# RWKV linear attention and a two-layer MLP on one core: the first ten units in another order on all engines

## The chip, the core and the metric

The kernel runs on one core of a Trainium2 chip. The core has five engines that run their own instruction queues and wait for each other by semaphores: TensorE (PE in the profile, with its weight loads as PEld), VectorE (DVE), ScalarE (ACT), GpSimd (POOL) and SyncE (SP), which here only starts transfers. ACT and POOL start transfers too. SBUF is the working memory, PSUM the memory that TensorE writes.

The metric is the device time of one execution, in microseconds (us). Three runs of the kernel before took 186.01, 186.36 and 188.03 us, median 186.36.

## What is computed

The reference is a linear attention with a decaying state, followed by two matrix products with a SiLU between them:

```python
# r, k, v: (4, 8, 768, 48) f32; w, u: (8, 48)
for t in range(768):
    cur = einsum('bhd,bhe->bhde', u[None] * kt, vt)
    y[:, :, t] = einsum('bhd,bhde->bhe', rt, state + cur)
    state = w[None, :, :, None] * state + einsum('bhd,bhe->bhde', kt, vt)
x = y.transpose(0, 2, 1, 3).reshape(3072, 384)
h = x @ w_in              # w_in (384, 2048)
out = (h * sigmoid(h)) @ w_out   # w_out (2048, 384)
```

## The kernel before

**Units.** The 768 time steps are cut into six chunks of 128. A unit is one batch entry in one chunk, for all eight heads, so there are 24 units; unit i is batch i mod 4 of chunk i div 4. Units 0 to 3 (chunk 0) start from a zero state and are worked one by one. From unit 4 on two units are worked as a pair, and each chunk is taken as two halves of 64 steps (`in_halves`), with an inner state between the halves.

**One unit.** Three loads of 192 KB bring r, k and v (`ld`, L72; buffers `rin`, `kin`, `vin`, eight of each). TensorE turns r and k (`turn_one`, L255, to the PSUM tile `att`, of which there are two in turn); VectorE multiplies them with powers of the decay (`decay_one`, L270: `rT`, `kT`); TensorE multiplies them (`product`, L322, or `product_halves`, L395); VectorE masks the products (`am`, L328 or L402); TensorE makes the outputs from them and from v cast to 16 bits (`v16`, L246), plus the part from the carried state (L338, L484 to L501, PSUM tile `yp`). The term with u is added apart: `ku` = k * r (L223), `rku_f` = ku * u (L228), its sum over the head's columns `rku` (L236, VectorE), and `vu` = v * rku (L241). VectorE adds `vu` to `yp` and gives the 16-bit `y` (L343). The state: `kc` = k times a decay (L231), TensorE sums kc times v (`sp`; `first_sums`, L359, for units 0 to 3, `sums`, L418, later), and VectorE, ACT and POOL build the states and their layouts (`st`, `s1`, `sdec`, `s0p`, `s0h` and so on). Before, all of `ku`, `rku_f`, `kc` and `vu` run on POOL and all `v16` on ACT.

**The MLP.** y is turned to `xT`, by TensorE and a copy for units 0 to 5 (L531, L535) and by a DMA on SP's queue later (L524). The first layer (L546) goes by blocks of 128 of the 2048 columns, `ft` = 0 to 15, with three matmuls for each; SiLU is on ACT (L555, `gT`). A piece is one such block for the chunk's four units (three 512-column matmuls), or two blocks for two units (six 256-column ones). The second layer (L568) makes 128 x 384 outputs for a unit in four parts of four matmuls; ACT (for the last chunk VectorE) copies them out (L574, L576) and SP stores them. The weights come by eight casting transfers that POOL starts: `i_q0` to `i_q3` (L83) each bring a quarter of w_in, that is four blocks, and `i_o0` to `i_o3` (L88) a quarter of w_out.

**The order.** The schedule is manual: every engine runs its instructions in the order in which the program names them. For the first units that order is written out as a string of words (`order`), each a step with a unit or block number: `T2` turns unit 2, `kT2` decays its k, `ku2`, `ru2` and `vu2` are the products, `rd2` the sum, `n2` or `m4` a mask, `V2` and `e2` outputs and `y`, `S0` sums of units 0 and 1, `Q4` of 4 and 5, `D4` products of the pair 4 and 5, `Z4` its outputs, `L2.0` a first-layer piece with `G2.0` as its SiLU, `lk5` a load, `H` a half piece of chunk 1. `6*spin` issues six matmuls on zeros (L168, tile `zs`). Before, the string ends ahead of the sums of units 6 and 7. Then a loop takes the pairs, and `fill(n)` puts n pieces or parts of the MLP from the list `fillers` between the steps of the attention. All PSUM tiles but `att` share four buffers in turn (tag `moe`), so a tile waits until the one four before it is read.

Of the kernel before, what the change touches and what calls it, by code (L numbers as in the profile page):

```python
# [15 lines left out]
def kernel(  # L16
# [129 lines left out]

    lnwT = cst.tile([PR, NP], FP)
# [96 lines left out]
    def cast_v(i):  # L244
        L(i)["v16"] = wrk.tile([128, H, D], F16, name="v16", bufs=4)
        nc.scalar.copy(out=L(i)["v16"], in_=vin[i % NIN])  # L246
# [304 lines left out]
    def l1_silu(sc, b0, nb, ft):  # L551
        if sc not in gts:
            gts[sc] = wrk.tile([128, NFT, B * C], F16, name="gT", bufs=2)
        m = B // nb
        nc.scalar.activation(out=gts[sc][:, ft:ft + m, b0 * C:(b0 + nb) * C], in_=hpss[b0, ft],  # L555
                             func=AF.Silu)
# [7 lines left out]
    def l2_mm(sc, b, part):  # L564
        if part == 0:
            opss[b] = ps.tile([128, HD], FP, name="ops", tag="moe", bufs=4)
        for ft in range(4 * part, 4 * part + 4):
            nc.tensor.matmul(opss[b], gts[sc][:, ft, b * C:(b + 1) * C], wout[:, ft, :],  # L568
                             start=(ft == 0), stop=(ft == NFT - 1))

    def store(sc, b):
        osb = wrk.tile([128, HD], FP, name="osb", bufs=3)
        if sc < NCH - 1:
            nc.scalar.copy(out=osb, in_=opss[b])  # L574
        else:
            nc.vector.tensor_copy(out=osb, in_=opss[b])  # L576
# [39 lines left out]
    def rest_first(sc):  # L616
        return [lambda ft=ft: l1(sc, 2, 2, ft) for ft in range(0, NFT, 2)]

# [6 lines left out]
    begun = second(0)  # L625
    halved = [lambda ft=ft: l1(1, 0, 2, ft) for ft in range(0, NFT, 2)]

    def piece(word, f):
        b0, ft = word.split(".")
        f(0, *blocks[b0], int(ft))  # L630

# [8 lines left out]
        "tab": silu_table, "clear": clear, "spin": lambda: None, "H": lambda: halved.pop(0)(),  # L640
    }
    unit_steps = {
        "T": turn, "rT": lambda i: decay_one(i, 0), "kT": lambda i: decay_one(i, 1),
# [11 lines left out]
        "cg": lambda i: zero_state(i, nc.gpsimd),  # L655
    }
    order = """
        ur kz0 id itr lr0 wy pd0 ak0 cz2 kz3 itc wr mk wx cz1 mh lnw eK cg3 lamK kz4 kz1 lk1
        id16 lr1 pd3 lr3 lk3 clear 6*spin lv0 cg0 lv1 kz7 lr2 ak2 ku0 lv3 lr5 kz2 lv2 ub pd1 lv4
        lr4 lk4 lv5 pd2 lk5 lk7 lr6 lk6 uc T0 1*spin T1 lr7 lv7 kT0 pa4 rT0 ru0 ku1  # L660
        v160 pd5 lv6 rT1 kz6 rd0 kT1 wb ru1 P0 n0 2*spin rd1 P1 vu0 lnwb T2 n1 v161 2*spin
        pd7 lamC lamH pa6 i_q0 V0 v162 tab rT2 e0 kT2 ku2 T3 1*spin yT0 V1 kz5 vu1 i_q1 ru2
        xTD0 e1 P2 yT1 kT3 rd2 rT3 ku3 xTD1 P3 ru3 n2 rd3 v163 n3 L0.0 vu2 kc0 1*spin G0.0
        vu3 V2 L0.2 V3 G0.2 L0.4 e2 i_q2 e3 kc1 yT2 yT3 S0 G0.4 xT2 xTD3 kc2 L0.6 L2.4 G0.6
        st0 L2.0 scA0 v164 kc3 L2.6 ku4 i_q3 v165 L2.2 T4 rT4 kT4 G2.4 ru4 G2.2 T5 G2.0 G2.6
        L4.8 G4.8 L4.10 kT5 G4.10 L4.9 kc4 ku5 S2 L4.11 rd4 rT5 st2 sc2 kc5 sd4 ru5 G4.9
        G4.11 rA4 vu4 i_o0 Q4 D4 rA5 s1_4 ku7 L4.12 rd5 vu5 m4 s2_4 G4.12 L4.13 G4.13 T6 Z4
        L4.14 G4.14 L4.15 z4 yT4 2*spin yT5 i_o2 i_o1 ku6 xT4 xT5 rT6 T7 G4.15 rT7 v167 sd6
        kT6 v166 ru6 lr8 kc6 kc7 H H rd6 i_o3 H vu6 lr9 rP7 rA6 sn4 H H lk8 lk9 sx4 lv9 lv8
        ru7 kT7  # L670
    """
    for word in order.split():
# [5 lines left out]
        elif word[0] == "L":  # L678
            piece(word[1:], l1_mm)
        elif word[0] == "G":  # L680
            piece(word[1:], l1_silu)
        else:
            unit_steps[word[:-1]](int(word[-1]))
    fillers.extend(halved + begun)

    for i in range(B + 2, NU, 2):
# [7 lines left out]
        if i == B + 2:  # L694
            bonus_sum(i + 1)
            bonus_v(i + 1)
# [3 lines left out]
        if i > B + 2 or sc < NCH - 1:  # L700
# [55 lines left out]
```

## Time and profile before

| | |
|---|---|
| median of three runs | 186.36 us |
| the profiled execution's own time | 186.19 us |
| its span, first to last instruction | 184.5 us |
| mean granted clock of TensorE | 0.998 |
| TensorE, VectorE, ScalarE, GpSimd busy | 177.5, 115.9, 106.8, 112.1 us |
| read from and written to HBM | 20.45 and 4.72 MB |
| a load of r, k or v, issue to landing (median) | 3.9, 4.5, 4.3 us |
| a quarter of w_in, of w_out, issue to landing (median) | 6.0, 6.7 us |

A row of the profile's groups has line, engine, operation, what is written from what, count, then the busy time in us with the mean of one in ns, and then the engine's idle time just before and what ended it. The chain is the work that ended last, followed back from the end: start, length, what. In the timeline a row is start and length in us, engine, line, operation. A busy matmul can be one that only stands in the pipeline, so where TensorE's time is at stake the steps from start to start say more than the durations.

### The profile page before, as it was taken

The page shows a single profiled execution, that of the slowest core. Times are in us where ns is not written, and L with a number is a line of the kernel's source. Part 1 is how long each engine was busy: PE and PEld are TensorE (multiplying, and loading weights), DVE is VectorE, ACT ScalarE, POOL GpSimd, SP SyncE. Part 2 cuts the span into 40 slices and gives each one's busy share as a digit, 9 for nine tenths or more (in the row PEclk, how much of TensorE's full clock was granted, in tenths as well). Part 3 has the DMA queues.
Part 4 walks back from the last instruction along what each step waited for, and adds up shares of the span by engine and source line. Part 5 has one row for each costly group of instructions (what it writes and reads, how often), then busy time and mean ns, then how long its engine had stood idle before and what let it go on. Part 6 is the DMA issues. An engine that isn't in the chain of part 4 may idle for free.

```text
span 184.5 us, 6822 instructions
## 1 busy us (share of the span) xinstructions
PE 177.5 (96%) x2913; PEld 117.2 (64%) x2913; DVE 115.9 (63%) x226; ACT 106.8 (58%) x209; POOL 112.1 (61%) x148
## 2 busy tenths in 40 slices
PE   7987998999999999999999999999999999999993
PEld 2565785688666976756657656657656566555563
DVE  4799729786885855895845985946974954000120
ACT  3462788599124694268694268694377692299200
POOL 7999999997999439639558567579169030000000
PEclk9999999999999999999999999999999999999999
DMA  5999999899596386386295396293396201410022
GB/s 95 235 211 210 167 216 195 151 221 230 100 190 198 89 168 138 87 171 174 46 176 130 87 182 163 48 217 88 87 187 159 46 4 49 125 43 0 0 88 85
DMA packets 88594, 24.24 MB, mean 131 GB/s; under 512 B 83314, under 2 KB 88052, under 8 KB 88564
## 3 DMA queue, kind: packets, MB, share of 16 engines
q1 hardware_dynamic: 83952, 20.19, 50.3%
q0 software_dynamic: 2176, 3.15, 10.2%
q10 hardware_dynamic: 2436, 0.46, 1.3%
q8 instruction: 23, 0.38, 0.8%
q14 instruction: 7, 0.06, 0.1%
HBM read 20.45 MB, written 4.72 MB: 136 GB/s over the span
## 4 chain that ended last, share of the span: by engine, by line
PE 73%; POOL 17%; DMA 6%; issue 2%; ACT 0%; POOLq 0%
PE ops L568 33%; PE hps L546 26%; DMA kin<-in_k_dram 6%; PE att L395 4%; PE att L255 4%; POOL ku L223 4%; POOL kc L231 3%; POOL rku_f L228 3%; POOL vu L241 2%; PE yp L492 2%; PE sp L418 2%; PE ops L593 1%; POOL win L83 1%; PE yp L501 1%; POOL wout L88 1%
## 5 line engine op out<-in xcount | busy, mean ns | idle before, releaser
L546 PE MATMUL hps<-xT,win 128*128 128x512 f16 (+1 forms) x360 | 66.3, 337 | 0.3 <-DMA win<-in_moe_w_in_dram 0.3
L555 ACT ACTIVATE gT<-hps 128x512 f16<-128x512 f32 x96 | 56.0, 597 | 14.1 <-PE hps L546 10.6
L568 PE MATMUL ops<-wout,gT 128*128 128x384 f16 x368 | 62.5, 326 | 0.0
L546 PEld LDWEIGHTS <-win 128*128 128x128 f16 x360 | 38.9, 114 | 21.3 <-DMA win<-in_moe_w_in_dram 0.4
L568 PEld LDWEIGHTS <-gT 128*128 128x128 f16 x368 | 35.2, 98 | 23.3
L241 POOL TENSOR_TENSOR vu<-vin,rku 128x384 f32<-128x384 f32 x24 | 19.6, 831 | 22.7 <-DVE rku L236 22.6
L223 POOL TENSOR_TENSOR ku<-kin,rin 128x384 f32<-128x384 f32 x24 | 24.1, 1003 | 11.6 <-DMA kin<-in_k_dram 11.5
L270 DVE TENSOR_TENSOR rT<-att,lamR 112x512 f32<-112x512 f32 (+1 forms) x40 | 26.9, 682 | 4.2 <-PE att L255 3.8
L574 ACT COPY osb<-ops 128x384 f32<-128x384 f32 x20 | 9.6, 479 | 34.1 <-issue 18.1
L343 DVE TENSOR_TENSOR y<-yp,vu 64x384 f16<-64x384 f32 (+1 forms) x34 | 18.9, 555 | 16.1 <-PE yp L501 8.0
L228 POOL TENSOR_TENSOR rku_f<-ku,u_bc 128x384 f32<-128x384 f32 x24 | 24.1, 1003 | 1.5
L231 POOL TENSOR_TENSOR kc<-kin,lamH 128x384 f16<-128x384 f32 x20 | 20.1, 1007 | 0.0
L270 DVE TENSOR_TENSOR kT<-att,lamK 112x512 f32<-112x512 f32 x24 | 16.3, 681 | 0.1
L246 ACT CAST v<-vin 128x384 f16<-128x384 f32 x24 | 11.3, 510 | 7.8 <-DMA vin<-in_v_dram 7.5
L435 DVE TENSOR_TENSOR s<-sp,sdec 112x384 f32<-112x384 f32 x10 | 5.6, 558 | 16.1 <-PE sp L418 16.1
L576 DVE COPY osb<-ops 128x384 f32<-128x384 f32 x3 | 1.7, 558 | 21.3 <-PE ops L568 21.3
L402 DVE TENSOR_TENSOR am<-att,maskH 128x1024 f16<-128x1024 f32 x10 | 12.2, 1219 | 1.1 <-PE att L395 1.1
L236 DVE TENSOR_REDUCE rku<-rku_f 128x8 f32<-128x384 f32 x24 | 12.4, 543 | 0.0
L395 PE MATMUL att<-rT,kT 48*64 48x64 f32 x640 | 11.9, 220 | 0.5 <-issue 0.5
L374 ACT CAST s1h<-s 48x384 f16<-48x384 f32 x16 | 8.1, 509 | 5.4 <-DVE s L435 5.2
L395 PEld LDWEIGHTS att<-rT,kT 48*64 48x64 f32 x640 | 10.6, 135 | 0.7 <-issue 0.7
L255 PE MATMUL att<-ident,rin 64*112 64x64 f32 x192 | 10.0, 223 | 0.4 <-DVE rku L236 0.4
(92 smaller groups left out, 175.0 us busy)
## 6 DMA issues: line engine op xcount, KB each, us to landing
rin<-in_r_dram SPq DMA_DIRECT2D x24, 192.0 KB, 3.9
vin<-in_v_dram SPq DMA_DIRECT2D x24, 192.0 KB, 4.3
out_dram<-osb SPq DMA_DIRECT2D x23, 192.0 KB, 2.7
kin<-in_k_dram SPq DMA_DIRECT2D x22, 192.0 KB, 4.5
win<-in_moe_w_in_dram POOLq DMA_DIRECT2D x4, 384.0 KB, 6.0
wout<-in_moe_w_out_dram POOLq DMA_DIRECT2D x4, 384.0 KB, 6.7
kin<-in_k_dram ACTq DMA_DIRECT2D x2, 192.0 KB, 3.7
xT<-y SPq DMA_TRANSPOSE x18, 2.3
```

The source lines that it names most:

```text
L223: eng.tensor_tensor(out=L(i)["ku"], in0=kin[i % NIN][:, :, 0:D], in1=rin[i % NIN][:, :, 0:D], op=ALU.mult)
L228: eng.tensor_tensor(out=L(i)["rku_f"], in0=L(i)["ku"], in1=u_bc, op=ALU.mult)
L231: eng.tensor_tensor(out=kc[i % NIN][:, :, 0:D], in0=kin[i % NIN][:, :, 0:D], in1=lamH if in_halves(i) else lamC, op=ALU.mult)
L236: nc.vector.tensor_reduce(out=L(i)["rku"], in_=L(i)["rku_f"], axis=mybir.AxisListType.X, op=ALU.add)
L241: eng.tensor_tensor(out=L(i)["vu"], in0=vin[i % NIN], in1=L(i)["rku"].unsqueeze(2).broadcast_to([128, H, D]), op=ALU.mult)
L255: nc.tensor.transpose(L(i)["t"][0:PR, y, x, p, :], flat[rows, 128 * p:128 * p + PR], ident[rows, rows])
L270: nc.vector.tensor_tensor(out=L(i)[key].rearrange("p g (y t) -> p y g t", y=2), in0=L(i)["t"][0:PR, :, x], in1=lam, op=ALU.mult)
L343: nc.vector.tensor_tensor(out=y16[a], in0=y[b, 0:HD], in1=vu[a], op=ALU.add)
L395: nc.tensor.matmul(a[o0:o0 + HC, j, e, p, :], kT[r0:r0 + D, p, HC * x:HC * x + HC], rT[r0:r0 + D, p, HC * x:HC * x + HC], start=True, stop ...
L546: nc.tensor.matmul(hps[:, f, :], win[(ft + f) // 4].rearrange("p q (t c) -> p q t c", c=4) [:, q, :, (ft + f) % 4], xts[sc][:, q, b0:b0 + ...
L555: nc.scalar.activation(out=gts[sc][:, ft:ft + m, b0 * C:(b0 + nb) * C], in_=hpss[b0, ft], func=AF.Silu)
L568: nc.tensor.matmul(opss[b], gts[sc][:, ft, b * C:(b + 1) * C], wout[:, ft, :], start=(ft == 0), stop=(ft == NFT - 1))
```

## The change

The string of words is replaced by a longer one. It now goes to the hand-over ahead of the sums of units 10 and 11, and the loop starts at unit 10 instead of 6 (`2 * B + 2`). All that the loop did for units 6 to 9, and the filler pieces between, now stand in the string: `N` and `U` are half pieces of chunk 1 with their SiLU, `M` a part of the second layer, `O` a copy with its store, `yD` the turning by DMA, `rV` and `rW` the decayed r in 16 bits. When the loop starts, five of the 16 second-layer parts of chunk 1 are done (`second(1)[5:]`).

New words put operations on other engines: `kuD`, `ruD`, `kcD`, `vuD` run these products on VectorE (ku of units 3, 6, 8, 10; rku_f of 0, 4, 6, 8, 11; kc of 2, 7, 8; vu of 6, 10, 11), `v16D` casts v on VectorE (units 4, 5, 7, 8, 11), `rD` casts r there (5, 6; before on ACT), `ca` zeroes one state tile by copies on ACT. Two of the matmuls on zeros stay of 15. Unit 0 is loaded, turned and multiplied ahead of the rest, the sums of units 0 and 1 stand between the outputs of unit 0 and those of unit 1, and unit 3 comes ahead of 2. Quarters of w_in are asked for in the order 0, 3, 1, 2. The dictionaries of PSUM tiles get the chunk's number as a key.

```diff
+    def zero_state_copy(n):
+        t = (carry_pairs + inner_pairs)[n]
+        for e in range(2):
+            nc.scalar.copy(out=t[:, e].rearrange("p g n -> p (g n)"), in_=idle[0:PR, 0:NP * PW])
...
-    def cast_v(i):
+    def cast_v(i, copy=nc.scalar.copy):
...
-        hps = hpss[b0, ft] = ps.tile([128, m, nb * C], FP, name="hps", tag="moe", bufs=4)
+        hps = hpss[sc, b0, ft] = ps.tile([128, m, nb * C], FP, name="hps", tag="moe", bufs=4)
...
+        "kcD": lambda i: decayed_k(i, nc.vector), "vuD": lambda i: bonus_v(i, nc.vector),
+        "kuD": lambda i: bonus_ku(i, nc.vector), "ruD": lambda i: bonus_rku(i, nc.vector),
+        "v16D": lambda i: cast_v(i, nc.vector.tensor_copy), "rD": cast_r,
...
     order = """
-        ur kz0 id itr lr0 wy pd0 ak0 cz2 kz3 itc wr mk wx cz1 mh lnw eK cg3 lamK kz4 kz1 lk1
-        id16 lr1 pd3 lr3 lk3 clear 6*spin lv0 cg0 lv1 kz7 lr2 ak2 ku0 lv3 lr5 kz2 lv2 ub pd1 lv4
-        lr4 lk4 lv5 pd2 lk5 lk7 lr6 lk6 uc T0 1*spin T1 lr7 lv7 kT0 pa4 rT0 ru0 ku1
-        v160 pd5 lv6 rT1 kz6 rd0 kT1 wb ru1 P0 n0 2*spin rd1 P1 vu0 lnwb T2 n1 v161 2*spin
...
+        lr0 id pd5 clear wx cz0 pd7 cg3 kz7 ur mk pd2 lr1 ub lk1 wr wy pd6 lr3 itr kz0 lv0 ak0
+        itc pa1 lk3 kz4 kz1 pa0 lnw Ta0 Tb0 kz2 cz1 lv1 lk2 ku0 eK lamK wb lr2 uc mh ku1 rT0 Ta1
+        Tb1 lnwb ruD0 v160 kT0 lamC rd0 lv2 v161 P0 kT1 ru1 rT1 n0 pa3 vu0 P1 2*spin Ta3 id16
+        ca2 rd1 n1 Tb3 lk5 lamH i_q0 kT3 lr4 kc0 kuD3 kc1 tab rT3 ku2 V0 S0 Ta2 V1 pa4 e0 v162
+        Tb2 st0 vu1 e1 lv3 yT0 ru3 scA0 P3 xT0 lr5 yT1 kc3 kT2 ru2 rT2 xT1 i_q3 rd3 P2 v163 n3
+        L0.0 L0.2 kz3 vu3 Ta5 V3 rd2 lk4 G0.0 n2 V2 i_q1 vu2 Ta4 G0.2 kcD2 S2 e3 yT3 e2 yT2 Tb5
+        st2 lv5 xT3 scA2 i_q2 ku5 lv4 Tb4 xTD2 ru5 L2.0 L2.2 lk6 L4.12 lr6 kT5 L4.13 G2.0 G2.2
...
-    fillers.extend(halved + begun)
-
-    for i in range(B + 2, NU, 2):
+    fillers.extend(second(1)[5:])
+
+    for i in range(2 * B + 2, NU, 2):
```

More of the change, by code (lines that the diff above doesn't have):

```diff
@@ L663 @@
[L663 to L668, printed above, removed]
@@ L699 @@
             decayed_k(n)
-        if i > B + 2 or sc < NCH - 1:
-            next_state(i)
+        next_state(i)
         fill(4)
@@ L710 @@
         if b:
-            fillers.extend((first(sc) if sc > 1 else rest_first(sc)) + second(sc))
+            fillers.extend(first(sc) + second(sc))
         for n in nxt:
```

63 lines of the change are left out of this document (39 added, 24 removed).

## The prediction

> **What bounds the kernel now.** I read the page's busy times first, then the chain that ended last in order of time, then the stretches of 5 us, then each engine's timeline up to 72 us.
>
> ```profile
> PE 177.5 (96%) x2913; PEld 117.2 (64%) x2913; DVE 115.9 (63%) x226; ACT 106.8 (58%) x209; POOL 112.1 (61%) x148
> ```
>
> 96% for PE counts matmuls that are only pipelined or waiting, so it doesn't say where time is lost. The chain does:
>
> ```profile
> 47.59 0.44 PE att L255 x8
> 48.03 7.91 PE ops L568 x48
> ...
> 66.40 3.25 PE ops L568 x20
> 69.65 0.37 PE sp L418 x32
> ...
> 89.05 4.66 PE hps L546 x21
> 102.70 4.66 PE ops L568 x28
> ```
>
> From 47.59 us on every piece is PE and each starts where the last ends. Two prices come from here: 4.66/21 = 0.222 us for one 512-column matmul of the first layer (0.67 us for a piece, which is three of these or six of 256 columns), and 4.66/28 = 0.166 us for one of the second layer (0.66 us for a part of four). The first `sp` piece of units 10 and 11 is at 69.65 us. There the rewritten order hands over to the loop, which is the same in both kernels, except that the new order has done five of the 16 second-layer parts of chunk 1, the old one four. So the whole change is worth: 69.65 + 0.65 minus the time at which the new kernel reaches that `sp`.
>
> ```profile
> 5.00:10.00 5.00, 5.00 (x72) 3.04 (x71) 4.04 (x14) 1.56 (x5) 4.86 (x9) 1.00 1.18 238
> 10.00:15.00 5.00, 4.37 (x88) 2.95 (x88) 5.00 (x9) 2.92 (x8) 4.93 (x8) 1.00 1.16 198
> 15.00:20.00 5.00, 3.93 (x90) 3.18 (x86) 5.00 (x10) 2.62 (x4) 4.92 (x6) 1.00 1.24 218
> 20.00:25.00 5.00, 4.68 (x62) 4.16 (x61) 2.41 (x5) 3.16 (x7) 4.98 (x6) 1.00 1.04 158
> ```
>
> (PE, PEld, DVE, ACT, POOL busy in each stretch, then granted clock, DMA share, GB/s.) From 5 to 20 us DVE and POOL are both full, and PE waits for them. From 20 us on DVE has room, POOL has none until 40 us. DMA is full to about 45 us.
>
> ```profile
> 2.97 2.77 PE L168 MATMUL zs<-idle 128*128 128x512 f16 x6
> 9.93 0.60 PE L168 MATMUL zs<-idle 128*128 128x512 f16 x2
> 18.57 0.85 PE L546 MATMUL hps<-xT,win 128*128 128x256 f16 x6
> ```
>
> The first useful first-layer matmul (piece 0.0) is at 18.57 us. The dummies before it step at 0.43 us early on and at about 0.2 us later.
>
> **The prize.** From 18.57 to 69.65 us are 51.1 us. The work in it, at the chain's dense prices: 32 first-layer pieces 21.3; 20 second-layer parts 13.2; turns of eight units 8 x 0.52 = 4.2; five pairs of sums at 0.37 = 1.9; three product pairs at 0.98 = 2.9; outputs of units 4 to 9, 0.83 + 0.83 + 0.65 = 2.3; two outputs and four turned y of units 2 to 5, 1.3. That is 47.1 us: 4 us of it are dummies and waits. The new order has one pair of sums less in it and one part more, 47.4. If piece 0.0 stays where it is and PE never waits, the `sp` comes at 66.0 us, and the gain is 69.65 + 0.65 - 66.0 = 4.3 us. Only an earlier piece 0.0 could give more.
>
> **The moved operations.** Up to the hand-over 15 two-input products go from POOL to DVE (four `ku`, five `rku_f`, three `kc`, three `vu`), and seven casts from ACT to DVE.
>
> ```profile
> L223 POOL TENSOR_TENSOR ku<-kin,rin 128x384 f32<-128x384 f32 x24 | 24.1, 1003 | 11.6 <-DMA kin<-in_k_dram 11.5
> L343 DVE TENSOR_TENSOR y<-yp,vu 64x384 f16<-64x384 f32 (+1 forms) x34 | 18.9, 555 | 16.1 <-PE yp L501 8.0
> ```
>
> On POOL such a product takes 1.0 us. No row has it on DVE; nearest is `y`, as wide, 0.555 us, whose one input lies in PSUM. With both inputs in SBUF beside a POOL that reads SBUF all the time, nothing in this trace says whether the two run freely: `eK`, the only such DVE operation (0.69 us), ran beside memsets. So the bounds are 0.47 us (the step from one `y` to the next instruction) and 0.555 plus one whole POOL operation, 1.56 us. I take 0.555 plus half a POOL operation, 1.05 us, while POOL is full, as either engine comes at a random moment of the other's instruction and both ends of the range are equally far; free running is a rival. The casts: 0.35 us (`xT`) to 0.62 (ACT's `rT`), I take 0.4 to 0.6. By the Trainium skill (SBUF — State Buffer, Who interferes with whom) a DVE instruction with two SBUF inputs and a GpSimd instruction that reads SBUF block each other for a whole instruction; no run shown here has that pair. By that rule the held-up value stands, without it the rival's.
>
> **The walk** (steps between starts on DVE: decay 0.60, mask 1.15, reduce 0.46, `y` 0.5).
> *To piece 0.0.* Old: 18.57. In the new order `rku_f` of unit 0 stands on DVE ahead of `kT` of unit 0 and waits for POOL's `ku` (k0 is now the fourth DMA of ACT's queue, not the third, and lands at about 6.4 instead of 5.89, so `ku` ends at 7.45). Free: products of unit 0 at 8.65 (old 8.90), masks to 13.0, two decays, `ku` of unit 3, `y0`, state copy, `y1`, two decays to 17.5, products of unit 2, piece 0.0 at 18.6: no gain, since DVE is as full as before. Held up: 0.25 for `rku_f` behind the half mask, 0.5 for `ku`: 19.4, a loss of 0.8.
> *To piece 2.0.* DVE has both masks, `kc` of unit 2, `y3`, `y2`, state copy and `xT2`: free 23.25, held up 24.5 (0.5 more for `kc`). PE's work there (two pieces, two half turns, outputs, sums, turned y, two half turns) is 3.6 us, so 1.0 or 1.5 are lost.
> *To piece 8.* It needs w_in quarter 2, now asked for last: POOL's order puts quarters 3, 1, 2 at 19.6, 21.4 and 23.5 us (18.5, 20.2, 21.9 free; old: 25.1, 14.1, 20.5). One alone takes 5.4 us to land; when queued, they land 2.8 us apart (w_out: 38.56, 41.39, 44.23). Quarter 3 lands at 25.1, before its use at 25.9; quarter 2 at about 31.2 (free 30.0), while PE gets there at 30.2 (29.0): 1.0 lost. The other loads fill the DMA as before, about 0.9 us each; r6 and k6 are there by 31, needed at 34.7.
> *To the end of chunk 0's first layer.* After the turns of units 6 and 7 DVE has `ku6` and four decays ahead of the products, then three `y` ahead of the turned y: 0.5 lost free, 1.0 held up (40.6 us). All of w_out is asked for from 38.7 on; the first part needs it at 48.7.
> *Units 6 to 9.* `kc7`, two casts, mask and `rku_f` of unit 6 stand before the inner state of units 6 and 7: outputs wait 1.15 held up, about 0.1 free. Then `vu6`, three `y`, `kc8`, `ku8`, `rku_f` 8, seven decays end at 59.1 (55.3 free) against PE's 58.9 (55.9): 0.1.
> Everything else added sits under PE: POOL's `vu7` and `ku9` ahead of the third w_out quarter (asked for at 43.7, needed at 53.4), the DMA transposes behind loads on SP (needed one pair later). ACT loses seven casts, gains a zeroing, and was busy for 24.7 of the first 40 us. v3 stands behind k5 and r4 now and lands at about 18.4 (12.84 before; the fourteenth load of before landed at 18.46), in time for unit 3's outputs at 20 us.
>
> **Sum.** Held up: 0.8 + 1.5 + 1.0 + 1.0 + 1.15 + 0.1 = 5.6 lost of the prize of 4.3: 1.3 to 1.4 us slower, on the profiled execution's own 186.19 us: **187.6 us** (the median of the runs is 186.36). Free: 1.0 + 1.0 + 0.5 + 0.1 = 2.6 of 4.3, a gain of 1.7: 184.5. A chip can tell about 1% (1.9 us) of this kernel from no change.
>
> **Rivals.**
> *DVE and POOL run freely*: **184.5 us**, from 183.4 if quarter 2 also lands in time. For it: DVE has 19 us idle up to 70 us (50.9 busy), the added 10.5 fit, and POOL loses 14 us of work in its full stretch. Against: the first 20 us, where DVE has no room.
> *The clock of TensorE*: the first dummies step at 0.43 us, the pair at 9.93 at half that, although the granted clock reads 1.00 throughout; only work in between can have done that. The change takes away 13 of 15 dummies, the six at 2.97 us above all, and PE waits for r0, k0, r1. If PE is still slow up to 20 us, two pairs of products (1.03 each) double, one before the masks and one before piece 0.0 (1.0 + 1.1), and part of that hides behind quarter 2; two slow pieces add 1.3. That decides once PE's work between 3 and 9 us is too sparse: **189.7 us**. The Trainium skill (TensorE: Matmul & The Clock Gate, Part 1) puts the release after about 3.4 us of sustained activity and half the clock before it; the dummies agree (0.43, later 0.2).
> *What PE gains DVE loses*: half of the moved operations meet an idle POOL (it waits for `rku` of unit 7 and for k9 after 38 us), and the waits cancel the prize: 186.2, no change.
>
> **The numbers.** Held up 0.45, own range 186.0 to 189.5; free 0.27; slow clock 0.16; no change 0.12. Faster than 184.5 needs about half of the free case and a little from others' errors in the walk: 0.25. Slower than 188.2: most of the slow clock, a third of the held-up case, 0.34 with errors of the walk, which sees no small waits. In between 0.41. The range, 183.4 to 190.4, takes in the free case with its best end and the slow clock with 0.7 on top.
>
> **What would show it.** Right: piece 0.0 at 19 to 20.5 us; DVE's two-input products above 0.56 us or late beside a busy POOL; DVE full from 5 to 40 us; a wait for `win` of about 1 us near 30 us; `sp` of units 10 and 11 near 71.7 us, and the same length after it. Wrong: products at 0.55 us with nothing queued and `sp` by 68.5 us; transposes and products of units 0 to 3 twice as long as here; or a loop after the hand-over that no longer runs PE piece to piece.

## The result, and the profile after

| | before | after |
|---|---|---|
| median of the runs | 186.5 us (4 runs) | 193.19 us (4 runs, 192.7 to 194.41) |
| ratio after/before, 95% interval | | 1.0354 [1.0277, 1.0431] |
| the profiled execution's own time | 186.19 us | 193.1 us |
| its span | 184.5 us | 190.6 us |

The changed kernel is 3.5% slower. The sign is as forecast; the size is not: 193.2 lies beyond 183.4 to 190.4. The busy times of the page after (to set against those of before):

```profile
PE 178.9 (94%) x2900; PEld 118.8 (62%) x2900; DVE 133.0 (70%) x242; ACT 107.3 (56%) x210; POOL 101.0 (53%) x132
```

VectorE has 17.1 us more to do, GpSimd 11.1 less. Of VectorE's 17.1 only some 10.7 are the work of the 22 operations (15 times 0.55 and 7 times 0.35, the times with nothing beside them). The chain of after in order of time (start, length, what):

```profile
32.11 1.49 PE hps L551 x6
...
45.26 2.69 DVE rku_f L233
47.95 0.48 DVE s L440
...
62.08 1.16 PE att L400 x64
...
70.39 2.98 DVE rku_f L233
73.38 0.27 DVE v L251
...
75.95 1.16 PE att L400 x64
```

Before, this chain is TensorE from 47.59 us on. Now VectorE carries most of it from 34.75 to 76 us, with two products `rku_f` of 2.7 and 3.0 us that take 0.55 where nothing is beside them. That the chain runs through VectorE does not mean that TensorE stood still all that time. What TensorE waited for, its own timeline names:

```profile
48.47 0.20 PE L489 MATMUL yp<-s0p,rT 112*64 112x96 f16 x1 [1.41 <-DVE s L440]
49.53 0.26 PE L489 MATMUL yp<-s1p,rT 112*64 112x96 f16 x2 [0.86 <-ACT s1p L375]
62.08 1.16 PE L400 MATMUL att<-rT,kT 48*64 48x64 f32 x64 [0.45 <-DVE rT L275]
75.95 1.16 PE L400 MATMUL att<-rT,kT 48*64 48x64 f32 x64 [0.62 <-DVE rT L275]
```

With two waits for `y` (0.30 at 40.50 and 0.15 at 52.00) that is 3.8 us from 34.75 to 76 us, and none between 62.08 and the sums of units 10 and 11. From 75.95 us on TensorE runs from piece to piece as before. The same stretches as were shown of before (length of the stretch, then PE, PEld, DVE, ACT and POOL busy, granted clock, DMA share, GB/s):

```profile
5.00:10.00 5.00, 3.88 (x44) 2.50 (x46) 3.18 (x7) 2.50 (x6) 3.58 (x5) 1.00 1.15 229
10.00:15.00 5.00, 5.00 (x88) 3.73 (x84) 4.02 (x6) 4.49 (x11) 4.98 (x7) 1.00 1.05 194
15.00:20.00 5.00, 3.90 (x110) 3.12 (x108) 5.00 (x10) 2.27 (x6) 5.00 (x6) 1.00 1.03 189
20.00:25.00 5.00, 4.34 (x78) 3.31 (x76) 5.00 (x8) 1.77 (x4) 4.88 (x8) 1.00 1.13 194
```

From 20 to 25 us VectorE, 2.41 us busy before, is full; from 10 to 15, where it was full, it now has 1 us to spare, because TensorE is late. TensorE's timeline of after has the three marks:

```profile
9.40 3.67 PE L327 MATMUL att<-rT,kT 48*64 48x128 f32 x64
20.12 1.50 PE L551 MATMUL hps<-xT,win 128*128 128x256 f16 x12
74.90 0.44 PE L423 MATMUL sp<-v,kc 64*64 64x48 f16 x32
```

The products of units 0 and 1 take 1.84 us each (1.09 before): TensorE, with no dummies ahead of it, is slow until about 13.9 us. Piece 0.0 starts at 20.12 (18.57). The sums of units 10 and 11 come at 74.90 (69.58 in before's timeline). Of the 6.9 us between the two profiled executions 1.55 are there by piece 0.0, 3.77 more by these sums, 0.8 more up to the end of the span (products of units 10 and 11 wait 0.62 for `rT`), and 0.8 lie outside the span (2.5 us after, 1.7 before).

Two measures are used below: the time of piece 0.0, and the **stretch** from there to the sums of units 10 and 11, 51.01 us before and 54.78 after. Both are TensorE's starts in the timeline of the profiled execution.

### The profile page after: what moved, and what is told of

It reads as the page before. It is cut to its first block, busy times and chain, and to the rows that moved or that the text cites. A ratio compares the mean times of both kernels' runs of the same rounds, so it can differ in the third digit from the quotient of the medians.

```text
span 190.6 us, 6771 instructions
## 1 busy us (share of the span) xinstructions
PE 178.9 (94%) x2900; PEld 118.8 (62%) x2900; DVE 133.0 (70%) x242; ACT 107.3 (56%) x210; POOL 101.0 (53%) x132
## 4 chain that ended last, share of the span: by engine, by line
PE 62%; DVE 19%; POOL 7%; DMA 7%; issue 2%; ACT 0%; ACTq 0%; DVEq 0%; POOLq 0%
PE ops L573 25%; PE hps L551 24%; DMA win<-in_moe_w_in_dram 5%; PE att L400 4%; PE att L260 4%; DVE rku_f L233 3%; DVE rT L275 3%; DMA kin<-in_k_dram 2%; DVE y L348 2%; DVE kT L275 2%; POOL vu L246 2%; POOL ku L228 2%; DVE rku L241 2%; POOL kc L236 2%; PE ops L598 1%
## 5 line engine op out<-in xcount | busy, mean ns | idle before, releaser
L560 ACT ACTIVATE gT<-hps 128x512 f16<-128x512 f32 x96 | 56.7, 597 | 17.8 <-PE hps L551 14.0
L246 POOL TENSOR_TENSOR vu<-vin,rku 128x384 f32<-128x384 f32 x21 | 18.8, 910 | 31.0 <-DVE rku L241 31.0
L228 POOL TENSOR_TENSOR ku<-kin,rin 128x384 f32<-128x384 f32 x20 | 20.6, 1031 | 13.4 <-DMA kin<-in_k_dram 13.2
L233 POOL TENSOR_TENSOR rku_f<-ku,u_bc 128x384 f32<-128x384 f32 x19 | 19.0, 1002 | 7.3 <-DVE ku L228 6.1
L236 POOL TENSOR_TENSOR kc<-kin,lamH 128x384 f16<-128x384 f32 x18 | 18.5, 1029 | 0.0
L260 PE MATMUL att<-ident,kin 64*112 64x64 f32 x192 | 9.8, 225 | 1.1 <-ACT lamK L191 1.1
L260 PE MATMUL att<-ident,rin 64*112 64x64 f32 x192 | 10.6, 232 | 0.0
```

Of the source, the lines that this page charges most:

```text
L228: eng.tensor_tensor(out=L(i)["ku"], in0=kin[i % NIN][:, :, 0:D], in1=rin[i % NIN][:, :, 0:D], op=ALU.mult)
L233: eng.tensor_tensor(out=L(i)["rku_f"], in0=L(i)["ku"], in1=u_bc, op=ALU.mult)
L236: eng.tensor_tensor(out=kc[i % NIN][:, :, 0:D], in0=kin[i % NIN][:, :, 0:D], in1=lamH if in_halves(i) else lamC, op=ALU.mult)
L246: eng.tensor_tensor(out=L(i)["vu"], in0=vin[i % NIN], in1=L(i)["rku"].unsqueeze(2).broadcast_to([128, H, D]), op=ALU.mult)
L260: nc.tensor.transpose(L(i)["t"][0:PR, y, x, p, :], flat[rows, 128 * p:128 * p + PR], ident[rows, rows])
```

## The experiments

The theory: 22 operations on VectorE wait beside a full GpSimd. The rivals: the clock of TensorE without its dummies; the new order itself; VectorE's own added work.

### The disputed cost by itself

*e1.* VectorE's products, casts and products that read PSUM, alone and beside six GpSimd products in a row.

```diff
+    x = meet("two", x, [tt] * 4)       # both inputs in SBUF
+    x = meet("cast", x, [cast] * 4)
+    x = meet("psum", x, [from_psum] * 4)
```

> This kernel leaves the whole computation out. It times four VectorE operations of 128 x 384 f32 beside a run of six GpSimd products of the same size that follow each other without a wait: first alone, then (a) products with both inputs in SBUF, (b) casts from SBUF to SBUF, (c) products with one input in PSUM. The first VectorE operation of each set waits for the first GpSimd product. Shut out for the run: in (a) the first operation ends only when GpSimd's six are done, about 5 us after it could start, and the other three take 0.5 each after that; (b) likewise if the cast uses the shared port; (c) 0.55 each, beside the run. Half an operation, as the prediction priced it: in (a) each operation takes 0.6 to 1.6 us and the two engines take turns. Free: 0.55 us in (a), 0.35 in (b), with GpSimd at 1.0 throughout.

VectorE's timeline in e1, alone and then beside GpSimd:

```profile
2.45 0.55 DVE L46 TENSOR_TENSOR alonetwob<-b 128x384 f32<-128x384 f32 x1
9.30 1.34 DVE L46 TENSOR_TENSOR twob<-b 128x384 f32<-128x384 f32 x1
16.78 1.15 DVE L51 CAST castb<-b 128x384 f16<-128x384 f32 x1
23.54 0.55 DVE L56 TENSOR_TENSOR psumc<-acc,b 128x384 f32<-128x384 f32 x1
```

The two engines take strict turns: a VectorE product of 0.55 us takes 1.34, a cast of 0.35 takes 1.15, and GpSimd's products stretch from 0.99 to 1.31. With one input in PSUM nothing happens. This fits the Trainium skill (SBUF — State Buffer, Who interferes with whom), by which a VectorE instruction with two SBUF inputs and a GpSimd instruction that reads SBUF shut each other out for a whole instruction. It does not explain the changed kernel, where most of the 22 operations took little more than alone (0.55, casts 0.35) and three took 2.3 to 3.1 us.

*e5, e9, e13.* So GpSimd was given the kernel's own forms. e5:

```diff
+    x = meet("A", x, [decay] * 6, [two] * 4)
+    x = meet("G", x, [state, decay, decay, plain, decay, plain], [mid, two, mid, cast, mid, two])
```

> The whole computation is left out: VectorE and GpSimd run against each other in seven groups, and the output is no result of the reference. GpSimd's runs now have the kernel's own forms: A six products kc (float16 out, rows of 64), B six sdec, C six products with rku broadcast, D kc and the memsets of kc in turn and a sdec at the end, E six kc, F six plain float32 products, G sdec, kc, kc, plain, kc, plain as around the operation of 3.07 us. VectorE has four two-input products in A to C; in D to G its operations with two inputs or casts stand between operations that read PSUM, so that each arrives in the middle of a GpSimd operation. If the turn-taking of the run before (1.33 us each, one GpSimd operation waited for) holds for every form, all contending VectorE operations take 1.0 to 1.4 us, in E to G 0.6 to 1.5 by when they arrive, and none reaches 2 us. If a form of GpSimd's keeps VectorE out over its end (kc with float16 out, or the memsets between), A, D, E or G show operations of 2 to 3 us and B, C, F do not. If it is the arrival in the middle that loses a turn, F shows 2 us as well.

Groups A and C showed turns (1.34 and 1.18), E and F the rest of one GpSimd operation (0.86); in B one product of four missed a turn (1.96); the cast groups stayed under 1.15. In G, where a `sdec` leads, the first product took 6.39 us: it got in only when GpSimd's run was over. e9 varied the moment of arrival, with and without a `sdec` at the head of the run:

```diff
+    for state in (False, True):
+        for again in range(2):
+            for delays in ([], [64], [128], [192], [256], [320], [384], [448], [512], ...):
+                x = meet(x, state, delays)
```

> The whole computation is left out: 48 small groups in which GpSimd runs five two-input products in a row and VectorE brings one two-input product (0.55 us alone), after reads of PSUM whose width sets the moment: it arrives between 0.1 and 1.1 us after the start of GpSimd's run, in 12 steps, each step twice. In the first 24 groups the run consists of plain float32 products, in the last 24 it begins with a sdec. If the moment of arrival decides who waits how long, the wait follows the steps in the same way in both halves and in both repeats: one remainder of a GpSimd operation for most moments (0.6 to 1.3 us for the product), and 3 us or more for a narrow window of moments near the end of a GpSimd operation. If the sdec ahead of it is what shuts VectorE out, the first half shows nothing above 1.5 us and the last half does. If it is chance, the repeats differ.

VectorE's timeline in e9, the second arrival of twelve, in the first half and in the second:

```profile
11.00 1.13 DVE L68 TENSOR_TENSOR two<-a,b 128x384 f32<-128x384 f32 x1
...
195.11 5.71 DVE L68 TENSOR_TENSOR two<-a,b 128x384 f32<-128x384 f32 x1
```

In 24 of 24 runs of plain products it took 0.66 to 1.35, falling by 0.07 for each step of arrival and jumping back after an end: it waits for the end of one operation. In 24 of 24 runs that a `sdec` began it took 4.85 to 5.84: passed over at every end until GpSimd had nothing left, also when it arrived after the `sdec` was over. Neither the moment nor chance decides; GpSimd's run does. e13 asked what it is in the run:

```diff
+        for x_op in (plain, state, wide, short, spread, decay, clean, cast, ask):
+            x = meet(x, [x_op] + [plain] * 4, 1)
```

> The whole computation is left out: 16 groups, done twice over, of a GpSimd run with VectorE's two-input product arriving 0.35 us after the run's start. In the first nine the run is one operation X and then four plain products: X is a plain product, a sdec (112 partitions, second input broadcast), the same on 128 partitions, a plain product on 112 partitions, vu (128 partitions, second input broadcast), kc (float16 out), the memset of kc, a cast of 48 partitions, the request of a DMA. Then a sdec twice ahead of plain products, a sdec with one plain product between, a sdec ahead of kc; and four runs with a sdec, a vu or a DMA request in the middle against five VectorE products. The run before showed 0.66 to 1.35 us in runs of plain products and 4.85 to 5.84 us, to the end of the run, in all 24 runs that a sdec begins. If the number of partitions does it, the plain product on 112 shuts VectorE out and the sdec on 128 does not; if the broadcast input does it, the sdec on 128 and vu shut it out and the plain product on 112 does not; if it is any change of form between neighbours, vu, the memset, the cast and the DMA request ahead of plain products do so too, and kc perhaps. A VectorE product takes 0.6 to 1.4 us where it is let in at the next end of an operation and 4.5 us or more where it is not.

Both repeats agreed within 0.02 us except after a DMA request (1.73 and 1.60). The product took 0.99 behind a plain product, 0.82 behind the 128-partition `sdec` and behind `vu`, 1.03 behind the plain product of 112 partitions, 0.99 behind `kc`; but 1.77 behind the `sdec`, 1.44 behind a cast, 1.6 to 1.7 behind a DMA request: there it was passed over at one end. None of the three answers expected came out clean, and the wait to the end of the run did not come back, though the run of `sdec` and four plain products looks like that of e9. What decides how many ends are missed stays open.

### Moving the operations back

*e2* returned four of the operations that were held up longest, the casts of r of units 5 and 6 and `rku_f` of units 6 and 11:

```diff
-  rD5 ... rD6 ... ruD6 ... ruDB
+  rA5 ... rA6 ... ru6 ... ruB
```

> The new kernel with the four VectorE operations that took longest beside GpSimd put back: rku_f of units 6 and 11 on GpSimd, the casts of r of units 5 and 6 on ACT. If being shut out by GpSimd's run is what delays the chain: the outputs of units 6 and 7 start at about 47 us instead of 49.5, the products of units 10 and 11 don't wait, the sums of units 10 and 11 come at about 72.5 instead of 74.9 us, and the time is about 190.5 us, 2.5 less than the new kernel. If the order of the steps costs the time, whoever runs them: within 0.7 us of 193.

It took 191.83 us, ratio 1.0312 [1.025, 1.0374], 1.4 less than the changed kernel, where 2.5 were expected; its runs (190.88 to 193.66) overlap with those of the changed kernel. TensorE no longer waited for `s` near 47 us. VectorE's timeline shows why the rest did not come:

```profile
27.41 2.41 DVE L233 TENSOR_TENSOR rku_f<-ku,u_bc 128x384 f32<-128x384 f32 x1
...
45.97 3.09 DVE L246 TENSOR_TENSOR vu<-vin,rku 128x384 f32<-128x384 f32 x1
...
68.08 3.85 DVE L251 CAST v<-vin 128x384 f16<-128x384 f32 x1
```

These three took 0.55, 1.28 and 0.35 in the changed kernel. Other moved operations were shut out in place of those taken away.

*e4* returned all 22, in the new order. *e7* moved the same 22 in the old order.

```diff
 e4:  -ruD0 kuD3 kcD2 rD5 ruD4 v16D4 ...     e7:  -ru0 ku3 kc2 rA5 ru4 v164 ...
      +ru0 ku3 kc2 rA5 ru4 v164 ...               +ruD0 kuD3 kcD2 rD5 ruD4 v16D4 ...
```

> The new order, but all 15 products back on GpSimd and all seven casts back on ACT, so that VectorE has no operation that reads SBUF beside GpSimd except as before. If the moves to VectorE cost the time: 187 to 190 us, with sums of units 10 and 11 at 69 to 72 us, though GpSimd has 14 us more to do. If the order costs it: 193 or more, with GpSimd full to 55 us and w_out asked for late.

> The old order, with the same 15 products on VectorE instead of GpSimd and the same 7 casts on VectorE instead of ScalarE. If the moves cost by themselves (VectorE held up while GpSimd runs), the time is 188 to 190 us, with VectorE operations of 1.3 to 3 us and waits of TensorE for VectorE in the first 76 us. If they cost only in the new order, where VectorE has no room, it is 185 to 187, GpSimd being the engine that was full in the old order until 45 us.

| | operations as before | 22 moved |
|---|---|---|
| old order | 186.36 | 200.46, ratio 1.0751 [1.0702, 1.08] (e7) |
| new order | 189.85, ratio 1.0208 [1.0157, 1.026] (e4) | 193.19 |

Each part costs by itself: the order 3.5 us, the moves 3.3 us in the new order and 14 in the old one, where at most 4 were expected. Not all of the 14 is time held up: in e7 TensorE, kept waiting, also ran slow again (18 first-layer matmuls at 50.97 took 4.03 us, 2.15 at its usual step, and the granted clock was 0.50 from 50 to 55 us). In e7 the longest waits of the moved operations lie in two runs of GpSimd that begin with a DMA request (at 21.50 and at 25.20 us):

```profile
23.65 2.35 DVE L231 TENSOR_TENSOR kc<-kin,lamC 128x384 f16<-128x384 f32 x1
...
26.39 4.64 DVE L246 CAST v<-vin 128x384 f16<-128x384 f32 x2
```

So the new order leaves VectorE better places for the 22 operations than the old one does, but not good enough ones.

### The same work on VectorE, less beside it

To tell waiting from work, GpSimd's side was made lighter and VectorE's left alone. *e10* and *e11* made every GpSimd product a memset, in the changed kernel and in e4:

```diff
+        if eng is nc.gpsimd:
+            return eng.memset(L(i)["ku"], 1.0)
```

> The changed kernel with its 22 operations on VectorE as they are, and each product left on GpSimd, and each sdec, replaced by a GpSimd memset of the same tile (about 0.2 to 0.45 us instead of 0.8 to 1.0, and with no input to read); what these products compute is left out. VectorE's own work is the same as in the changed kernel. If the moves cost 3.3 us because VectorE is held up by GpSimd's products, its operations take 0.55 and 0.35 (up to 0.8 at most), and the kernel comes to within 1 us of the next one. If they cost because VectorE simply has 10 us more to do in a stretch in which it is full, it stays 2.5 to 3.3 us above the next one.

> The new order with the 15 products on GpSimd and the 7 casts on ScalarE (189.85 us in full), with the same replacement: every product and sdec on GpSimd is a memset, so what they compute is left out, those 15 included. It is the one to compare the run before with: the same order and dummies, no operation held up, and 10 us less work for VectorE. Both theories expect 187.5 to 189.5 here, by what GpSimd's lateness costs this order (1.5 us of waits for kc in the run without the replacement); slower than 190 would mean that the dummies and the order cost more than was taken.

Ratios 1.0345 [1.0266, 1.0425] and 1.0397 [1.0348, 1.0447]: no difference that the moves could have made, but this pair does not settle it, since both became slower than e4. GpSimd, with nothing to wait for, asked for the last three w_in quarters between 13.3 and 16.1 us (19.4 to 22.7 in the changed kernel), and TensorE then waited for r, 5.8 us in e11. What it did show: beside memsets all 15 moved products took 0.55 us.

*e14* and *e15* left out only five `kc`, the ones beside VectorE's three longest waits:

```diff
-  kc5 ... kc4 ... kc9 ... kcB kcA
```

> The changed kernel with five of GpSimd's products left out: kc of units 4, 5, 9, 10 and 11, which stand where VectorE's three longest waits were (2.27 us at 27.61, 2.77 at 45.19, 3.07 at 70.31). What they compute is left out: the sums of those units use an older kc or zeros, so the output is not the reference's. VectorE keeps all 22 moved operations. None of the five is waited for by the path of the changed kernel, so only what they did to VectorE is taken away. If those waits are what the moves cost, the three operations take about 0.6 to 1.3 us, the outputs of units 6 and 7 wait at least 1 us less, the sums of units 10 and 11 come 1.5 to 3 us before 74.90, and the time is 190.2 to 191.7. If VectorE's own added work is the cost, or the wait moves on to the next operation each time, it is 192.5 to 193.5.

> The same five kc left out of the kernel with the 15 products on GpSimd and the 7 casts on ScalarE (189.85 us with them), as the measure for the run before: what they compute is left out. No VectorE operation is held up here, so it should stay at 189.2 to 190.1; less would mean that GpSimd's work itself was late in this order, and only what the run before gains beyond that is the hold-up's.

e14 took 191.86 us, ratio 1.0285 [1.0232, 1.0338], e15 190.15, ratio 1.0212 [1.0177, 1.0248]: the gap of 3.3 us between changed and moved back shrinks to 1.7, and e15 stays where e4 was. VectorE's timeline of e14, the three operations of 2.27, 2.77 and 3.07 us:

```profile
28.10 0.45 DVE L311 CAST rT<-rT 112x512 f16<-112x512 f32 x1
...
44.85 1.81 DVE L233 TENSOR_TENSOR rku_f<-ku,u_bc 128x384 f32<-128x384 f32 x1
...
69.03 1.14 DVE L233 TENSOR_TENSOR rku_f<-ku,u_bc 128x384 f32<-128x384 f32 x1
```

*e17* and *e18* made all GpSimd products of units 4 to 11 memsets, and kept the w_in requests where they were:

```diff
+        return eng is nc.gpsimd and 4 <= i < 12
```

> The changed kernel with each product that GpSimd makes for units 4 to 11 replaced by a memset of the same tile (what they compute is left out); the products of units 0 to 3, each sdec, the DMA requests and all 22 moved operations stay, so that the w_in requests, which an earlier run moved with its memsets, keep their moments. In that earlier run no VectorE operation was held up beside memsets (0.55 and 0.42 us). If waiting beside GpSimd's products makes the whole 3.3 us between the changed kernel and the one with everything moved back, of which leaving out five products showed half, this run comes to within 0.8 us of the next one, whatever time that has. If the other half is VectorE's own 10 us of added work, it stays 1.3 to 2 us above it.

> The same replacement, units 4 to 11, in the new order with the 15 products on GpSimd and the 7 casts on ScalarE: the measure for the run before. What the replaced products compute is left out. VectorE is not held up here in full (189.85 us) either; 188.5 to 190.2 is expected, less only by what GpSimd's products are late for in this order.

Ratios 1.0226 [1.0165, 1.0286] and 1.038 [1.0291, 1.047]. The whole times do not compare: in e18's profiled execution TensorE was slow again from 18 to 25 us (units 2 and 3 multiplied in 1.97 us each), and piece 0.0 came at 22.60, its twelve matmuls in 2.62 us instead of 1.50. So a second, shorter stretch is set beside the first: from the start of piece 2.0, the next first-layer work, where TensorE is at full speed in all of these:

| to the sums of units 10 and 11, us | from piece 0.0 | from piece 2.0 |
|---|---|---|
| before | 51.01 | |
| all 22 moved back, with dummies (e8) | 51.92 | 46.13 |
| all 22 moved back, without five `kc` (e15) | 51.39 | 46.00 |
| all 22 moved back, units 4 to 11 memsets on GpSimd (e18) | 51.47 | 46.13 |
| changed | 54.78 | 49.57 |
| changed, five `kc` left out (e14) | 53.01 | 47.80 |
| changed, units 4 to 11 memsets on GpSimd (e17) | 52.42 | 47.49 |

(e4's own stretch, 53.16, is left aside: 21 first-layer matmuls at 25.90 took 4.95 us there, 3.44 in the others.) From piece 2.0 on the moves cost 3.4 us (49.57 less 46.13). TensorE's named waits account for 2.9 of them: it waits 0.82 for w_in, 0.30 and 0.15 for `y` and 1.41, 0.86 and 0.45 behind VectorE in the changed kernel, and 0.93 for w_in and 0.21 for `y` in e8. With five `kc` gone on both sides 1.8 of the 3.4 are left (e14 and e15), with memsets on both sides 1.4 (e17 and e18). What is left beside memsets is of another kind. TensorE's timeline of e17 names 0.28 us for w_in, 0.36 behind a cast of v that had itself waited 0.94 for its load, and this wait for a load of k:

```profile
47.54 0.44 PE L271 MATMUL att<-ident,kin 64*112 64x64 f32 x8 [0.76 <-DMA kin<-in_k_dram]
```

In e18, where TensorE gets there 3 us later, none of the three is there. VectorE's own work is the same in the changed kernel, e14 and e17. So waiting beside GpSimd's products is at least 2.0 of the 3.4 us, and no row names a wait that VectorE's own added work alone would explain.

### The dummies

*e3* put six dummies back in the changed kernel, *e6* took 13 of 15 from the old one, *e8* gave e4 sixteen, *e16* gave the changed kernel the same sixteen.

```diff
 e3:   id pd5 clear +6*spin wx cz0
 e6:   clear -6*spin lv0;  T0 -1*spin T1;  n0 -2*spin rd1;  T3 -1*spin yT0;  kc0 -1*spin G0.0;  yT4 -2*spin yT5
 e8 and e16:  clear +6*spin;  rT0 +1*spin;  P0 +4*spin;  ku2 +1*spin;  P3 +1*spin;  ahead of S2 +3*spin
```

> The new kernel with the six matmuls on zeros back behind the clearing of att, as the kernel before has them. If TensorE is slow because these are gone: the products of units 0 and 1 take about 2.1 us together instead of 3.67, the masks come 1 us earlier, piece 0.0 starts at about 19.1 instead of 20.1 us, and the time falls by 0.3 to 1.0 us (part of it is lost again in the wait for quarter 2 of w_in): 192.2 to 192.9. If the slow products have another cause: 3.67 us and 193.2 again.

> The old order and its old engines, with 13 of its 15 dummy multiplications taken away and nothing else. If the slow TensorE clock is what the order costs (the 3.6 us that are left when all products and casts are moved back), the products of units 0 and 1 take 1.5 to 2 us instead of 1.09, the transposes and first pieces are slow up to 20 us and more, piece 0.0 comes 1 to 1.5 us later than 18.57, and the time is 187.7 to 189.7 us. If the dummies do not matter (the clock comes up by itself before TensorE is the limit), it is 185.9 to 186.6.

> The new order with all 15 products on GpSimd and the 7 casts on ScalarE (189.85 us without more), and 16 dummy multiplications put back where TensorE is idle: 6 after the clearing of the banks, 1 before the transposes of unit 1, 4 after the product of unit 0, 1 before the outputs of unit 0, 1 after the product of unit 3, 3 before the sums of units 2 and 3. If the slow clock makes the order's 3.6 us, the products take 1.09 throughout, piece 0.0 comes at 18.6 to 19.3 and the time is 186.5 to 188. If the order costs by its late w_in quarters and its later first-layer pieces, it stays at 189 to 190.3.

> The changed kernel as it is, with 16 dummy multiplications at the places where they took 1.2 us off the kernel with everything moved back (6 after the clearing, 1 before the transposes of unit 1, 4 after the product of unit 0, 1 before the outputs of unit 0, 1 after the product of unit 3, 3 before the sums of units 2 and 3). If the six dummies of an earlier run failed (194.15 us) because the clock fell back in the sparse stretch behind them, the products take 1.09 us here up to piece 0.0 and the time is 191.6 to 192.6. If an earlier TensorE only brings the masks and casts of VectorE to worse moments beside GpSimd, it stays at 193 to 194.5, with the clock up.

| | time, us | ratio to before | piece 0.0 |
|---|---|---|---|
| e3, changed + 6 | 194.15 | 1.043 [1.0393, 1.0468] | 21.45 |
| e6, before - 13 | 186.94 | 1.0035 [1.0004, 1.0066] | 20.28 |
| e8, e4 + 16 | 188.62 | 1.0116 [1.0067, 1.0166] | 20.23 |
| e16, changed + 16 | 193.9 | 1.0419 [1.0371, 1.0466] | 20.12 |

In the old order the slow start brings piece 0.0 1.7 us later, as the rival said (e6: both products 1.84 us), but only 0.7 us of it is left at the end. In e4 sixteen dummies are worth 1.2 us. In the changed kernel they are worth nothing (193.9 against 193.19, with runs that overlap), and VectorE's timelines show why, first e16, then after:

```profile
12.15 1.22 DVE L333 TENSOR_TENSOR am<-att,maskM 128x1024 f16<-128x1024 f32 x1
13.29 0.68 DVE L275 TENSOR_TENSOR kT<-att,lamK 112x512 f32<-112x512 f32 x1
13.89 1.96 DVE L228 TENSOR_TENSOR ku<-kin,rin 128x384 f32<-128x384 f32 x1
15.78 0.68 DVE L275 TENSOR_TENSOR rT<-att,lamR 112x512 f32<-112x512 f32 x1
```

```profile
13.16 1.23 DVE L333 TENSOR_TENSOR am<-att,maskM 128x1024 f16<-128x1024 f32 x1
14.70 0.69 DVE L275 TENSOR_TENSOR kT<-att,lamK 112x512 f32<-112x512 f32 x1 [0.31 <-PE att L260]
15.31 0.55 DVE L228 TENSOR_TENSOR ku<-kin,rin 128x384 f32<-128x384 f32 x1
15.77 0.68 DVE L275 TENSOR_TENSOR rT<-att,lamR 112x512 f32<-112x512 f32 x1
```

With a fast TensorE the mask comes 1.0 us earlier, `ku` of unit 3 meets GpSimd and waits 1.4 us, and `rT` starts at 15.78 instead of 15.77. The slow clock and the waiting stand in for each other. e3 had both: `ku` waited (2.04 at 13.62), and the clock fell back at about 16.8 us, so that units 2 and 3 took 1.97 each. The dummies alone do not set the moment at which TensorE becomes fast: e4 and e18 begin like the changed kernel, without dummies ahead of the first products, and the products of unit 0 took 1.09 there (at 7.98 and 7.92), while the next ones were slow (1.49 and 1.97 at 11.4).

### Taking out waits

*e12* is e8 with three waits of TensorE taken out of its order, the one for the late w_in quarter among them:

```diff
-  L4.8 ... L2.6        G0.2 kc2 3*spin S2        xT1 i_q3
+  L2.6 ... L4.8        G0.2 1*spin S2            xT1 kc2 i_q3
```

> The kernel with everything moved back and 16 dummies (188.62 us), with three waits of TensorE taken out of its order: the piece that needs the third w_in quarter (0.93 us of waiting) changes places with one of the second quarter, kc of unit 2 goes on GpSimd ahead of the request of the fourth quarter instead of behind the second (0.74 us), and two dummies of 0.22 us go. If these waits are what the order still costs, the time is 186.8 to 187.4. If piece 0.0 at 20.2 instead of 18.57 is what it costs, and the waits only move on, it is 188.2 to 188.8.

It took 189.17 us, ratio 1.0144 [1.0112, 1.0176], no better than e8. The waits moved on: TensorE now waits 1.1 for `y` of unit 2 (its `vu` ends at 24.2), and 0.5 and 0.7 for w_in. A piece of another quarter that is moved forward meets a quarter that has not landed either.

So of the order's 3.5 us the dummies return 1.2. Where the other 2.3 lie, e8's own timeline shows. Its sums of units 10 and 11 come 2.6 us later than before's: 1.66 are there by piece 0.0, though no operation is moved and the products of units 0 and 1 take 1.09 us, and 0.9 come in the stretch behind. TensorE waits:

```profile
15.68 0.40 PE L364 MATMUL sp<-v,kc 128*64 128x48 f16 x14 [1.12 <-POOL kc L236]
```

The new order puts `ku` of unit 3 between the `kc` of units 0 and 1. Given back to GpSimd, it takes 1.00 us there, and the `kc` of unit 1 comes behind it (14.64). In the stretch e8's waits add up to 1.9 us (0.74 for another `kc`, 0.93 for w_in, 0.21 for `y`), before's to 1.0. That the `ku` is what makes piece 0.0 late in e8 was not tried by a run without it.

No version here beats the kernel before. The nearest with the new order is e8, 188.62.

## Why the prediction was wrong

**Right.** The mechanism of the likeliest case: moved operations held up beside a busy GpSimd, DVE full from 15 to 30 us and again from 35 on (though not from 5 to 15, where it was idle for 1.8 and 1.0 us), piece 0.0 between 19 and 20.5 us. The late quarter 2: it landed at 32.06 (forecast 31.2) and TensorE waited 0.82 (1.0 forecast). All cover named for the steps at no cost held: the w_out quarters landed by 53.31, ahead of use.

**The step that failed most: the prize of 4.3 us.** The sum was 5.6 lost of a prize of 4.3. The new order was to bring the sums of units 10 and 11 to 66.0 us if piece 0.0 stayed where it was and TensorE never waited, and the whole to 184.5 with the moved operations running freely. With nothing moved, so nothing more held up than before, the new order takes 189.85 (e4), 188.62 (e8) and 189.17 us (e12): 2.3 to 3.5 us slower than before, where the sum has a gain. No run shows the moved operations running freely; the nearest are these, 4 to 5 us above 184.5. Three parts of the prize can be named.

- "4 us of it are dummies and waits" was a remainder of prices, not a sum of rows. Before's timeline names 1.0 us of waits in that stretch (0.29, 0.51 and 0.23) and about 0.65 of dummies. The 0.51 among them is idle time in which TensorE waited for nothing that the profile shows. The rest of the 4 us was no waiting.
- Of this rest 0.66 us is a part that was not counted. Before has 21 second-layer parts ahead of these sums, not 20: five of chunk 1, as the new kernel has.
- For the same reason the credit of 0.65 for the hand-over was wrong. The same second-layer work follows these sums in both kernels, 16 matmuls and then 28, and the end of the span follows the sums by 114.9 us before and 115.7 after.

That leaves about 1.65 us of steps that cost more than their dense price; which ones is open. e8 shows the same: its stretch is 51.92 us where 47.4 were forecast, and its named waits and dummies make up only some 2.5 of the 4.5 between. An estimate from before's rows puts the prize at about 2 us: 51.0 less the waits, the dummies and one pair of sums (0.37) leaves 49.0. On top of that came the 1.66 us by piece 0.0, which the free case had at 18.6; no version of the new order has it before 19.88 (e12).

**The second step: "0.555 plus half a POOL operation, 1.05 us".** As a mean it was not far off: the five `rku_f` took 1.50, the four `ku` 0.61, the three `vu` 0.79, the three `kc` 0.81, together 14.7 us for 15, 0.98 each. The total came out too: held up less free was forecast at 187.6 less 184.5, 3.1 us, and undoing the moves gave 3.3. That is luck, since as a model it was wrong. A wait is nothing, or one GpSimd operation, or several, and the few long ones stood on the path. The outputs of units 6 and 7 waited 1.41 and 0.86 instead of 1.15 because one `rku_f` took 2.77, while the 1.3 that the walk put down for it ahead of piece 2.0 (0.8, and 1.5 instead of 1.0) do not show: the changed kernel starts that piece at 25.33, e8 and e15 at 26.02 and 25.66. Casts were priced without any wait; those of r took 2.27 and 1.06. The `rku_f` of 3.07 us did not delay the sums of units 10 and 11, for which TensorE names no wait; it made the products behind them wait 0.62.

**The sums.** Forecast 71.7 us for the sums of units 10 and 11, measured 74.90. By the walk's marks: at the end of chunk 0's first layer 0.75 of the 3.2 us (41.35 against 40.6), outputs of units 6 and 7 1.1, the wait of units 8 and 9 for `rT` 0.35. The other 1.0 falls mostly between the outputs of units 6 and 7 and the products of units 8 and 9, where only a wait of 0.15 for `y` is named; the cause of the rest is open. The whole miss, 193.1 against 187.6 us, is these 3.2, the credit of 0.65, 0.8 up to the end of the span and 0.8 outside it.

**Piece 0.0.** 0.8 lost was forecast for the held-up case, 1.55 came, by the other rival's cause: masks 1.0 us late behind slow products. e16, fast at the start, shows the held-up case at the same 1.55, and e8, with neither slow products nor moved operations, comes as late (20.23) by a third way, its `kc` on GpSimd. The clock rival named the right row but put the price at its end (189.7); in the changed kernel undoing it gained nothing.

**Not foreseen at all**: 0.8 us more outside the span. The changed kernel, e3, e14 and e16 have 2.3 to 3.4 us there, before, e4, e8, e12 and e15 1.6 to 1.8; but e2 has runs of both kinds. Why is open.

## What to carry to other kernels

An operation with two SBUF inputs, or a cast, that moves from GpSimd or ScalarE to VectorE must be priced by what GpSimd does at that moment, and by the worst wait that was seen, not by half an instruction: look at who stands behind it in VectorE's queue, and give it an input in PSUM or a stretch in which GpSimd is idle. Before an order is credited with "waits that go", add up the waits that the timeline names. Undo an order and its moves separately, and together with a start-up that is late: here two causes of the same 1.4 us hid each other.

## What the runs showed of the hardware

- VectorE and GpSimd take turns by whole instructions: 1.34 and 1.31 us beside each other, 0.55 and 0.99 alone (e1). Casts from float32 to float16 do so too (1.15, alone 0.35). Reads of PSUM and GpSimd's memsets leave VectorE alone (0.55).
- A waiting VectorE instruction can be passed over at the end of a GpSimd instruction: at one end behind a cast, a DMA request or a `sdec` (e13), and at every end, up to 5.84 us in e9 and 6.39 in e5, in runs with a `sdec` at their head. It is the same each time the same run is repeated; the rule was not found.
- TensorE's speed at the start follows the work given to it: products of 1.09 us at 8.90 with seven dummies ahead (before), 1.84 up to 12.9 us with none (after), 1.97 again at 17 to 21 us after a sparse stretch (e3). It is not the same in every execution without dummies: 1.09 at 7.98 in e4 and 7.92 in e18. The granted clock reads 1.00 in the first 20 us of after, the slow start included, but 0.50 in later slow stretches (17 to 20 us of e3, 15 to 25 us of e18). The Trainium skill (TensorE: Matmul & The Clock Gate, Part 1) names a window of about 3.4 us of activity for either change; here TensorE worked at half speed from 2.97 to about 13.9 us in the changed kernel, with transposes and small products most of the time, so the window alone does not tell when it ends.
